# HGRN2 attention and a maxout FFN on one core: the order of weight copies, loads, packing and stores on two DMA queues, and other rooms for the weight sums

## The chip, the core and the metric

The kernel runs on one core of a Trainium2 chip. The metric is the device time of one execution in microseconds (us), the median of several runs. A core has a matrix engine (TensorE, here PE; its weight loads are shown as PEld), a vector engine (VectorE, DVE), a scalar engine (ScalarE, ACT), a general engine (GpSimd, POOL) and a synchronising engine (SyncE, SP). Each engine takes its instructions strictly in its own order. DMAs are issued by an engine as instructions in that order too; SPq and ACTq are the names in the profile for the queues of SP and ACT.

## The reference

```python
def _attn_ref(q, k, v, f_logit):            # 4 batches, 8 heads, 768 steps, 48 features
    f = 1.0 / (1.0 + np.exp(-f_logit))
    state = np.zeros((B, H, D, D))
    for t in range(S):
        state = f[:, :, t, :, None] * state + np.einsum('bhd,bhe->bhde', k[:, :, t], v[:, :, t])
        y[:, :, t] = np.einsum('bhd,bhde->bhe', q[:, :, t], state)

def _moe_ref(x, w1, w2, w3, w_out):         # x: 3072 x 384; w1..w3: 384 x 768; w_out: 768 x 384
    h = np.maximum(np.maximum(x @ w1, x @ w2), x @ w3)
    return h @ w_out
```

The output of the attention, transposed to tokens by 384 features, is the input x of the second part. The four weights are handed in as 64-bit floats and brought to 32 bits on the chip.

## The kernel before

The sequence is cut into chunks of 64 steps. One unit u holds one chunk of two batches (128 tokens) with all eight heads, so there are 24 units (0 to 23); the state of each pair of batches is carried from unit u to unit u + 2. Four units make a group g of 512 tokens, for which the FFN is run. The attention of unit u and the FFN of the group before it are woven together by hand: a loop over u calls the attention's steps, and between them `fill(ns)` draws so many nanoseconds of matrix work from a generator of the FFN. What is written first comes first on its engine; nothing is reordered.

**A unit's attention.** From unit 6 on (`BY_ROWS = 6`) the gates f, the keys k and the queries q are loaded for two units at once: `load(8)` fetches f, k and q of units 8 and 9, eight DMAs for each of the three (L183). `load_v` fetches v of one unit in two DMAs (L164). `sigmoids(u)` (ACT, L311) makes the gates from f. `scan(u)` (DVE, L329) forms the running products of the gates. `after(u)` turns k (DVE, `kt`, L296), copies the ends (POOL, L339) and multiplies (POOL, `kh`, L340). `before(u)` scans again (L347), turns q (DVE, `qt`) and multiplies (POOL, `qh`, L351). `carry(u)` (POOL, L357) decays the state. On PE follow `pairs(u)` (k against q, L392), `values(u)` (L411), `sums(u)` (the new state, L436, added by DVE in L444) and `finish(u)` (the part of the state, L500). `finish` copies the result in three pieces into the group's tile `xT` (ACT, L506). The tile has a fourth part whose rows belong into gaps of the first three: `pack` moves them there with two DMAs (L519), once for units 0 to 2 of a group and once for the last.

**The FFN of group 0** (`ffn_first`) works with plain products while the weights still arrive and are rounded to 32 bits (`round_to`; ACT, DVE and POOL). When all three are there, `place` copies the second and third, minus the first, from `w_in[1]` and `w_in[2]` into the tiles `placed[0]` and `placed[1]`, in the row order that `xT` has (ten DMAs for each, L454 and L461). `linear` multiplies the first weight with `w_out` on PE (L776); the product is copied by ACT (L780), and placed by ten more DMAs from `w_nat` to `w_lin`. `outputs(i)` for i = 0 to 3 then makes the four output tiles (PE, L563), each in one of the two PSUM banks of the pool `ps_f`, copied out by ACT (L567) and stored by two DMAs (L555).

**The FFN of groups 1 to 5** (`ffn`) saves products by working on sums and differences of halves. It needs `w_sum` and one difference of the placed weights (`mix_in`, four POOL instructions of 128 x 768), `w_mix` of `w_out` (`mix`, four of 128 x 576), `x_mix` of `w_lin` (`mix_x`, five of 128 x 192), and for each group the sums of its inputs (`sums_of_x`, five of 128 x 256, L854). `placed[2]` serves as `w_sum`, `w_in[2]` holds `w_mix`. The PE products of these parts stand in L870 and L631.

**DMAs and their counters.** Every DMA, whichever engine issues it, counts its completion on one of eight counters. The counter is chosen when the program is built, in the order in which the builder expects the DMAs to run. A DMA is issued only when the one before it on the same counter has landed; the issuing engine waits for that in front of the DMA instruction, beside whatever the data demands.

Of the kernel before, what the change touches and what calls it, by code (L numbers as in the profile page):

```python
# [9 lines left out]
FP32 = mybir.dt.float32  # L10
# [3 lines left out]
ALU = mybir.AluOpType  # L14
# [41 lines left out]
def kernel(  # L56
# [33 lines left out]
    def fast():  # L90
        ctx = ExitStack()
        with ctx:
# [455 lines left out]
            def new_top(w):  # L548
                return work.tile([128, TOK], FP32, name="top")[:, 0:w]

            def store(u, o):
                c, bp = divmod(u, 2)
                for a in range(2):
                    t0 = (2 * bp + a) * S + c * C
                    nc.sync.dma_start(out=out[t0:t0 + C, :], in_=o[a * C:(a + 1) * C, :])  # L555

            def outputs(hm, xT, i):
                p = bank()
                t = slice(i % 2 * UT, (i % 2 + 1) * UT)
                terms = [(hm[:, j, i * UT:(i + 1) * UT], w_out[:, j, :]) for j in range(NJ)]  # L560
                terms += [(by_halves(xT)[:, i // 2, k, t], w_nat[:, k, :]) for k in range(NK)]
                for n, (lhsT, rhs) in enumerate(terms):
                    nc.tensor.matmul(p[:, 0:DM], lhsT=lhsT, rhs=rhs, start=(n == 0), stop=(n == NJ + NK - 1))  # L563
                    if n % NK == NK - 1:
                        if n == NJ + NK - 1:
                            o = o_four[:, i]
                            nc.scalar.copy(o, p[:, 0:DM])  # L567
                            store(i, o)
                        yield NK * DM * COLUMN


# [2 lines left out]

            HJ, HD = NJ // 2, DM // 2
            corner = lambda k, n: w_out[:, k::2, n * HD:(n + 1) * HD]
            w_mix = [corner(0, 1)] + [w_in[2][:, :, n * HD:(n + 1) * HD] for n in range(4)]
            x_mix = [w_lin[:, 0, HD:]] + [w_mix[4][:, n] for n in range(2)] + [keep.tile([128, HD], FP32, name="mix")]
            s_mix = [w_in[1][:, n, :].rearrange("q (jj t) -> q jj t", jj=HJ) for n in range(NK)]
            s_last = keep.tile([128, HALF], FP32, name="s_last")  # L580
# [1 line left out]

            def mix(n):

                dst, x, y = ((w_mix[2], corner(1, 1), corner(0, 1)), (w_mix[0], corner(0, 1), corner(0, 0)),
                             (w_mix[1], corner(1, 1), w_mix[0]), (w_mix[3], corner(1, 0), w_mix[1]))[n]
                nc.gpsimd.tensor_tensor(dst, x, y, op=ALU.subtract)

            def mix_x(n):

# [172 lines left out]
            def turn(j):  # L763

                p = ps_f.tile([128, TOK], FP32, name="p")
                piece = w_in[0][:, :, j * 128:(j + 1) * 128]
                for a in range(NK):
                    nc.tensor.transpose(p[:, a * 128:(a + 1) * 128], piece[:, a, :], ident)
                nc.scalar.copy(piece, p[:, 0:DM].rearrange("q (a c) -> q a c", a=NK))
                yield DM * COLUMN  # L770
# [15 lines left out]
            def ffn_first(xT):  # L786
                hm = new_hm()
                steps = [(j, slice(n * HALF, (n + 1) * HALF)) for n in range(2) for j in range(J_HALF)]
                steps += [(j, slice(0, TOK)) for j in range(J_HALF, NJ)]
                n_step = 0  # L790
                for j, t in steps:
                    w = t.stop - t.start
                    for i in (1, 2):
                        p = yield from product(xT, j, i, t)
                        if i == 1:
                            nc.scalar.copy(hm[:, j, t], p)
                        else:
                            nc.vector.scalar_tensor_tensor(hm[:, j, t], hm[:, j, t], 0.0, p, op0=ALU.max, op1=ALU.max)
                        round_to(ROUNDED[n_step])
                        load_weights(2, rounded[0] - 1)  # L800
                        yield (1 if w == TOK else NK) * w * COLUMN
                        n_step += 1
                        if n_step in TURNED:
                            yield from turn(TURNED[n_step])
                for a in range(NK):
                    if a < 2:
                        for n in range(2 * NK + 2):
                            place(placed[a].bitcast(FP32), w_in[a + 1], n)
                    for cost in linear(a):
                        round_to(rounded[0] + 1)  # L810
                        yield cost
                for n in range(2 * NK + 2):
                    place(w_lin, w_nat, n)
                made = iter([lambda n=n: mix_in(n) for n in range(4)] + [lambda: mix(0)])
                for i in range(GRP):
                    for n, cost in enumerate(outputs(hm, xT, i)):
                        if i or n:
                            next(made, lambda: None)()
                        if i == GRP - 1 and n == 1 and 1 in packed:
                            sums_of_x(1)  # L820
                        if i == GRP - 1 and n == 2:
                            for k in range(1, 4):
                                mix(k)
                        yield cost


# [1 line left out]


            w_two = [t.bitcast(FP32) for t in placed[0:2]]  # L830
            w_sum = [placed[2].bitcast(FP32)[:, n] for n in range(NK)]

            def mix_in(n):

# [23 lines left out]
            def inputs_by_pairs(g, hm, xT):  # L858
# [57 lines left out]
                def fourth(n):  # L916
                    into(A[n], n, w_two[1][:, 1], t4)
                    yield COST
                    into(A[n], n, w_two[1][:, 2], t5)
                    nc.vector.scalar_tensor_tensor(out(n, 0), out(n, 0), 0.0, two(A[n]), op0=ALU.max, op1=ALU.max)  # L920
                    nc.vector.scalar_tensor_tensor(out(n, 1), out(n, 1), 0.0, u3, op0=ALU.max, op1=ALU.max)  # L921
                    sums_of_hm(hm, n)
                    if g == 1:
                        for i in ((0, 1), (2, 3, 4), ())[n]:
                            mix_x(i)
                    yield COST

                yield from start(0)
# [52 lines left out]
            with tc.manual_schedule():  # L981
# [78 lines left out]
                for u in range(GRP, NU):  # L1060
                    n = u + 1
                    part = EARLY if u < 2 * GRP else PART
                    if n == BY_ROWS:
                        scan(n)
                    fill(part)
                    keys(u)
                    keys_by_blocks(u, 2)
                    if u > GRP:
                        finish(u - 1, xT)
                        if u % GRP == 3:  # L1070
                            pack(0, 2, xT)
                        elif u % GRP == 0:
                            pack(3, 3, xT)
                    if u % GRP == 0:
                        if u > GRP:
                            packed[u // GRP - 1] = xT
                            pending.append(ffn(u // GRP - 1, xT))
                        xT = x_tiles[u // GRP % 2]
                    pairs(u)

                    if u + 2 <= BY_ROWS:
                        load(u + 2)
                    if BY_ROWS <= u + 3 < NU and u % 2:
                        load(u + 3, one, "fkq" if u % GRP == 1 else "f")
                    if u + 2 < NU:
                        load_v(u + 2)
                    keys_by_blocks(u, 3)
                    if n < NU:
                        if n < BY_ROWS:
                            sigmoids(n)  # L1090
                        if n != BY_ROWS:
                            scan(n)
                    check_range(u - CHECKS, 0)
                    fill(part)
                    if n < NU:
                        after(n)
                        before(n)
                    fill(part)
                    if BY_ROWS < u + 2 < NU and u % GRP == 0:
                        load(u + 2, one, "k")  # L1100
                    values(u)
                    if n < NU:
                        carry(n)
                    check_range(u - CHECKS, 1)
                    fill(part)
                    if BY_ROWS < u + 2 < NU and u % GRP == 0:
                        load(u + 2, one, "q")
                    keys_by_blocks(n, 0)
                    fill(part - 1000 if u < 2 * GRP else part)
                    keys_by_blocks(n, 1)  # L1110
                    check_range(u - CHECKS, 2)
                    if u + 2 >= CHECKS:
                        check_load(u + 2 - CHECKS)
                    if BY_ROWS <= u + 2 < NU:
                        sigmoids(u + 2)
                fill(PART)
                finish(NU - 1, xT)
# [270 lines left out]
```

## Time and profile before

| | us |
|---|---|
| median of 3 runs | 415.52 (415.25 to 416.81) |
| the profiled execution | 416.47 |
| its span in the profile | 414.6 |
| PE busy | 397.8 (96% of the span) |
| DVE, POOL, ACT busy | 290.8, 245.2, 178.7 |

The span is the time from the first to the last instruction that the profiler saw; 1.9 us of the profiled execution lie outside it. Times inside the profile are counted from the span's start. A row such as `80.68 1.13 ACT L506 COPY xT<-y 128x256 f32<-128x256 f32 x3 [2.92 <-PE y L500]` says that three copies of line 506 began at 80.68, took 1.13 us from the first's start to the last's end, and that ACT had stood idle for 2.92 us until PE's line 500 released it. For SPq the duration is the time that issuing took; the time to landing comes on top.

### The profile page before, as it was taken

The numbers are of one execution on the slowest core, as the hardware profiler recorded it, in microseconds if no ns is written. First come the engines' busy times: TensorE is split into PE (matmuls) and PEld (weight loads), VectorE is DVE, ScalarE is ACT, GpSimd is POOL, SyncE is SP. The second block draws the span as 40 slices with busy tenths as digits, with TensorE's granted clock in tenths as the row PEclk, the third lists the DMA queues.
The fourth block names the chain that finished last, engine by engine and source line by source line (L and its number), as shares of the span: only waits on it lengthen the run. The fifth ranks groups of instructions, "written<-read, shape, count | busy, mean of one in ns | idle before, by whom it ended". The sixth has DMA issues, their size and how long they took to land.

```text
span 414.6 us, 11546 instructions
## 1 busy us (share of the span) xinstructions
PE 397.8 (96%) x4598; PEld 332.4 (80%) x4598; DVE 290.8 (70%) x569; ACT 178.7 (43%) x412; POOL 245.2 (59%) x270
## 2 busy tenths in 40 slices
PE   4988999999999999999999999999999999999995
PEld 4766775566668889998889988889988899988984
DVE  6987897996695899898888976988894550002500
ACT  2478786511223531444541354533345324576210
POOL 2189694730989887487496376667466860435700
PEclk9999999999999999999999999999999999999999
DMA  8989987677356767377625376724473011541002
GB/s 170 237 261 273 250 231 93 86 143 159 83 104 96 122 114 132 70 118 89 137 78 104 52 117 86 163 64 80 71 146 96 2 55 44 148 136 60 0 21 62
DMA packets 181562, 47.21 MB, mean 114 GB/s; under 512 B 160448, under 2 KB 179200, under 8 KB 181504
## 3 DMA queue, kind: packets, MB, share of 16 engines
q1 hardware_dynamic: 178032, 45.62, 54.0%
q10 hardware_dynamic: 3472, 0.81, 0.9%
q8 instruction: 37, 0.61, 0.6%
q14 instruction: 21, 0.17, 0.1%
HBM read 37.75 MB, written 4.72 MB: 102 GB/s over the span
## 4 chain that ended last, share of the span: by engine, by line
PE 76%; DVE 6%; SPq 5%; POOL 3%; DMA 3%; ACT 3%; issue 2%; ACTq 0%; POOLq 0%; DVEq 0%
PE p L870 16%; PE p L631 14%; PE tr L870 13%; PE tr L631 11%; PE p L537 6%; PE p L563 3%; PE y L411 3%; PE y L500 2%; PE p L776 2%; SPq L174 2%; DMA raw<-in_moe_w_dram 2%; PE a L392 2%; PE y L436 2%; DVE ks L382 2%; SPq L164 1%
## 5 line engine op out<-in xcount | busy, mean ns | idle before, releaser
L382 DVE STREAM_TRANSPOSE ks<-kh 32x128 f32<-32x128 f32 x256 | 77.4, 302 | 11.9 <-POOL kh L340 7.7
L870 PE MATMUL tr<-xT,placed 128*128 128x256 f32 x300 | 72.6, 385 | 0.3 <-DVE hm L913 0.3
L870 PEld LDWEIGHTS tr<-xT,placed 128*128 128x128 f32 x300 | 55.7, 190 | 9.3 <-ACT hm L878 1.2
L870 PE MATMUL p<-xT,placed 128*128 128x256 f32 x180 | 45.1, 382 | 0.3 <-POOL xT L854 0.3
L339 POOL COPY ends<-r 128x8 f32<-128x8 f32 x24 | 9.8, 407 | 48.5 <-DVE r L329 48.5
L870 PEld LDWEIGHTS p<-xT,placed 128*128 128x128 f32 x180 | 33.7, 190 | 5.3 <-POOL xT L854 0.7
L537 PE MATMUL p<-xT,w_in 128*128 128x256 f32 (+1 forms) x108 | 33.9, 458 | 3.0 <-POOL w_in L745 2.2
L329 DVE TENSOR_TENSOR_SCAN r<-gate,from_one 128x520 f32<-128x520 f32 x24 | 31.5, 1314 | 6.1 <-ACT gate L308 3.0
L340 POOL TENSOR_TENSOR kh<-kt,r 128x512 f32<-128x512 f32 x18 | 30.1, 1671 | 7.6 <-DVE kt L296 6.2
L639 DVE TENSOR_TENSOR o<-tr,w_in 128x384 f32<-128x384 f32 (+1 forms) x11 | 5.7, 521 | 38.6 <-PE tr L631 35.1
L347 DVE TENSOR_TENSOR_SCAN prod<-gate,from_inv 128x520 f32<-128x520 f32 x24 | 32.1, 1336 | 0.0
L603 POOL TENSOR_TENSOR w_in<-hm 128x256 f32<-128x256 f32 x15 | 11.1, 739 | 34.9 <-DVE hm L921 32.2
L506 ACT COPY xT<-y 64x256 f32<-64x256 f32 (+1 forms) x60 | 22.1, 369 | 19.2 <-PE y L500 18.1
L870 PE MATMUL p<-w_in,placed 128*128 128x256 f32 x120 | 30.0, 379 | 0.0
L913 DVE TENSOR_TENSOR hm<-tr,hm 128x512 f32<-128x512 f32 x15 | 10.3, 688 | 26.6 <-PE tr L870 19.7
L537 PEld LDWEIGHTS p<-xT,w_in 128*128 128x128 f32 x108 | 19.5, 190 | 11.8 <-issue 6.0
L636 ACT COPY w_in<-p 128x384 f32<-128x384 f32 x15 | 7.2, 478 | 46.0 <-PE p L631 46.0
L631 PE MATMUL p<-w_in,hm 128*128 128x192 f32 x120 | 25.4, 335 | 1.1 <-ACT w_in L636 1.1
L258 POOL TENSOR_TENSOR w_in<-top_bits,rest_bits 128x384 uint32<-128x384 uint32 x18 | 21.8, 1218 | 7.6 <-DVE top_bits L252 4.7
L280 ACT ACTIVATE raw<-top_bits 128x384 f32<-128x384 f32 x48 | 25.2, 526 | 0.4
L870 PEld LDWEIGHTS p<-w_in,placed 128*128 128x128 f32 x120 | 22.8, 190 | 3.1
L631 PE MATMUL tr<-w_out,w_in 128*128 128x192 f32 x120 | 24.4, 326 | 0.0
(159 smaller groups left out, 907.6 us busy)
## 6 DMA issues: line engine op xcount, KB each, us to landing
raw<-in_moe_w_dram SPq DMA_DIRECT2D x24, 384.0 KB, 3.8
v_ld<-in_v_dram SPq DMA_DIRECT2D x48, 96.0 KB, 3.2
placed<-in_moe_w_dram SPq DMA_DIRECT2D x12, 384.0 KB, 5.4
out_dram<-o SPq DMA_DIRECT2D x46, 96.0 KB, 2.2
placed<-in_moe_w_out_dram SPq DMA_DIRECT2D x6, 384.0 KB, 6.3
f_ld<-in_f_logit_dram SPq DMA_DIRECT2D x36, 64.0 KB, 3.4
k_ld<-in_k_dram SPq DMA_DIRECT2D x36, 64.0 KB, 2.5
q_ld<-in_q_dram SPq DMA_DIRECT2D x36, 64.0 KB, 2.5
```

Of the source, the lines that this page charges most:

```text
L258: nc.gpsimd.tensor_tensor(dst, by(top), by(rest), op=ALU.add)
L280: nc.scalar.activation(over, size, AF.Relu, scale=(-1 / HI_MIN, 1.0)[step - 1], bias=(1.0, -HI_END * (1 - 2.0 ** -24))[step - 1], accum_ou ...
L329: nc.vector.tensor_tensor_scan(r[:, 0:LEN][:, ::-1], flat(gate)[:, ::-1], flat(from_one)[:, ::-1], 1.0, op0=ALU.mult, op1=ALU.max)
L340: (nc.vector if u < BY_ROWS else nc.gpsimd).tensor_tensor(kh.rearrange("p h a t -> p a h t"), kt, by_batch(r[:, 1:LEN + 1].rearrange("p (x ...
L347: nc.vector.tensor_tensor_scan(flat(prod), flat(gate_tiles[u % 2]), flat(from_inv[u % 2]), 1.0, op0=ALU.mult, op1=ALU.max)
L382: nc.vector.transpose(ks[n * 32:(n + 1) * 32, :, par, e0:e0 + 32], kh[p0:p0 + 32, :, a, t0:t0 + 32])
L411: nc.tensor.matmul(y[o:o + DP, a, hp * C:(hp + 1) * C], lhsT=v_ld[s, 2 * hp + par, :], rhs=d["at"][s, par, hp, :], start=(hp == 0), stop=F ...
L506: nc.scalar.copy(xT[o, :, t0 + a * C:t0 + (a + 1) * C], y[i, a, 0:HP * C].rearrange("p (h t) -> p h t", h=HP))
L537: nc.tensor.matmul(p if w < TOK else p.rearrange("p (two t) -> p two t", two=2), lhsT=w_in[i][:, kt, j * 128:(j + 1) * 128], rhs=x[:, t.st ...
L563: nc.tensor.matmul(p[:, 0:DM], lhsT=lhsT, rhs=rhs, start=(n == 0), stop=(n == NJ + NK - 1))
L631: nc.tensor.matmul(b[:, p * HD:(p + 1) * HD], lhsT=x, rhs=w, start=id(b) not in begun, stop=True, skip_group_check=True)
L870: nc.tensor.matmul(b[:, j * HALF:(j + 1) * HALF], lhsT=w[:, (2 * n + j) * 128:(2 * n + j + 1) * 128], rhs=x, start=begin and j == 0, stop= ...
```

## The change

- In `ffn_first` the placing of both weights stands ahead of all of `linear` (before: each ahead of its own `linear(a)`). `mix(0..2)` and `mix_in(0..2)` are made during `linear(1)` and `linear(2)`, `mix_in(3)` at the first output, `mix_x` at outputs 2 and 3 (before: while group 1's inputs were multiplied), `mix(3)` at the last one.
- The rooms are swapped: `w_mix` lies in `placed[2]`, `w_sum` in `w_in[2]`. The second difference of `w_out` is formed from the first, by an addition.
- The stores of group 0's four outputs, and the packing of group 1's tile (at units 7 and 8), are issued by ACT instead of SP.
- `load(8)` moves from unit 5 to unit 6: f after `pairs(6)`, k and q and v of unit 8 after `values(6)`. `sigmoids(8)` moves from the end of unit 6 to unit 7, ahead of `scan(8)`.

```diff
-            def store(u, o):
+            def store(u, o, queue=nc.sync):
...
-                    nc.sync.dma_start(out=out[t0:t0 + C, :], in_=o[a * C:(a + 1) * C, :])
+                    queue.dma_start(out=out[t0:t0 + C, :], in_=o[a * C:(a + 1) * C, :])
...
-                            store(i, o)
+                            store(i, o, nc.scalar)
...
-            w_mix = [corner(0, 1)] + [w_in[2][:, :, n * HD:(n + 1) * HD] for n in range(4)]
+            spare = placed[2].bitcast(FP32).rearrange("q k c -> q (k c)")
+            w_mix = [corner(0, 1)] + [spare[:, n * NK * HD:(n + 1) * NK * HD].rearrange("q (k c) -> q k c", k=NK)
+                                      for n in range(4)]
...
-                dst, x, y = ((w_mix[2], corner(1, 1), corner(0, 1)), (w_mix[0], corner(0, 1), corner(0, 0)),
-                             (w_mix[1], corner(1, 1), w_mix[0]), (w_mix[3], corner(1, 0), w_mix[1]))[n]
-                nc.gpsimd.tensor_tensor(dst, x, y, op=ALU.subtract)
+                dst, x, y = ((w_mix[2], corner(1, 1), corner(0, 1)), (w_mix[1], w_mix[2], corner(0, 0)),
+                             (w_mix[3], corner(1, 0), w_mix[1]), (w_mix[0], corner(0, 1), corner(0, 0)))[n]
+                nc.gpsimd.tensor_tensor(dst, x, y, op=ALU.add if n == 1 else ALU.subtract)
...
+                for a in range(2):
+                    for n in range(2 * NK + 2):
+                        place(placed[a].bitcast(FP32), w_in[a + 1], n)
                 for a in range(NK):
-                    if a < 2:
-                        for n in range(2 * NK + 2):
-                            place(placed[a].bitcast(FP32), w_in[a + 1], n)
-                    for cost in linear(a):
-                        round_to(rounded[0] + 1)
+                    for n, cost in enumerate(linear(a)):
+                        round_to(len(pieces))
+                        if a:
+                            (mix, mix_in)[a - 1](n)
                         yield cost
...
-                made = iter([lambda n=n: mix_in(n) for n in range(4)] + [lambda: mix(0)])
                 for i in range(GRP):
                     for n, cost in enumerate(outputs(hm, xT, i)):
-                        if i or n:
-                            next(made, lambda: None)()
+                        if i == 0 and n == 0:
+                            mix_in(3)
+                        if (i, n) in ((2, 2), (3, 0)):
+                            for m in ((0, 1), (2, 3, 4))[i - 2]:
+                                mix_x(m)
...
                         if i == GRP - 1 and n == 2:
-                            for k in range(1, 4):
-                                mix(k)
+                            mix(3)
...
-            w_sum = [placed[2].bitcast(FP32)[:, n] for n in range(NK)]
+            w_sum = [w_in[2][:, n] for n in range(NK)]
...
-                    if g == 1:
-                        for i in ((0, 1), (2, 3, 4), ())[n]:
-                            mix_x(i)
...
                         finish(u - 1, xT)
+                        queues = act if u <= 2 * GRP else one
                         if u % GRP == 3:
-                            pack(0, 2, xT)
+                            pack(0, 2, xT, queues)
                         elif u % GRP == 0:
-                            pack(3, 3, xT)
+                            pack(3, 3, xT, queues)
...
-                    if BY_ROWS <= u + 3 < NU and u % 2:
-                        load(u + 3, one, "fkq" if u % GRP == 1 else "f")
-                    if u + 2 < NU:
+                    if u == BY_ROWS:
+                        load(u + 2, one, "f")
+                    elif u + 1 != BY_ROWS:
+                        if BY_ROWS <= u + 3 < NU and u % 2:
+                            load(u + 3, one, "fkq" if u % GRP == 1 else "f")
+                    if u + 2 < NU and u != BY_ROWS:
                         load_v(u + 2)
...
-                        if n < BY_ROWS:
+                        if n < BY_ROWS or n == BY_ROWS + 2:
                             sigmoids(n)
...
                     values(u)
+                    if u == BY_ROWS:
+                        load(u + 2, one, "kq")
+                        load_v(u + 2)
...
-                    if BY_ROWS <= u + 2 < NU:
+                    if BY_ROWS <= u + 2 < NU and u != BY_ROWS:
                         sigmoids(u + 2)
```

## The prediction, made before the changed kernel was run

> **What bounds the kernel now.** I read the page first: PE is busy for 96% of the span, so a change that leaves PE's work alone can save only PE's waits or add new ones. Then the list of who waited for whom on PE: between 60 and 340 us hardly any wait is long. Then the chain that ended last, between 105 and 155 us, and the timelines of SP, ACT and PE around it.
>
> ```profile
> PE 397.8 (96%) x4598; PEld 332.4 (80%) x4598; DVE 290.8 (70%) x569; ACT 178.7 (43%) x412; POOL 245.2 (59%) x270
> ```
>
> The chain runs over PE, except here:
>
> ```profile
> 109.89 0.13 SPq L519
> ...
> 118.70 2.00 DMA out_dram<-o
> 120.70 1.99 DMA xT<-xT
> 122.75 0.09 issue
> 122.84 0.74 POOL xT L854
> ```
>
> SP's queue is full: from 40 to 163 us one DMA follows another. The packing of unit 7, whose data ACT has copied by 109.9, is issued at 120.0; POOL waits for it, and PE's product of group 1 waits for POOL.
>
> ```profile
> 124.43 1.13 PE L870 MATMUL p<-xT,placed 128*128 128x256 f32 x4 [0.30 <-POOL xT L854]
> 131.32 0.71 DVE L296 STREAM_TRANSPOSE kt<-k_ld 128x512 f32<-128x512 f32 x1 [3.53 <-DMA q_ld<-in_q_dram]
> ```
>
> DVE waits for the keys of unit 10 for the same reason. How much it costs PE: from `pairs(9)` at 122.42 to `pairs(13)` at 183.94 are 61.52 us, over the next four units 59.62. The difference, 1.9 us, is all that a relief of this queue can give; of it I find 1.3 us in gaps between PE's products at 123.8, 138.0, 154.1 and 162.
>
> Two lines show the rule that matters most below: an engine's queue stands still behind a DMA that waits, here for up to 17 us.
>
> ```profile
> SPq L519 <- ACT xT L506: 64.7, 9, 17.0
> 94.59 1.14 ACT L506 COPY xT<-y 128x256 f32<-128x256 f32 x3 [1.55 <-PE y L500]
> 99.09 0.48 ACT L567 COPY o<-p 128x384 f32<-128x384 f32 x1 [3.36 <-PE p L563]
> 105.97 2.10 PE L563 MATMUL p<-w_out,hm 128*128 128x384 f32 x6
> 108.00 0.67 PE L500 MATMUL y<-qh,state 48*48 48x64 f32 x32
> 108.49 0.65 PE L392 MATMUL a<-qh,kh 48*64 48x64 f32 x32
> ```
>
> The second is `finish(6)`, after which unit 6 can be packed; the last is `pairs(8)`, which follows `finish(7)` with no gap. `qh(8)` is ready at 108.39, so `pairs(8)` has no slack at all.
>
> **What the Trainium skill says.** DMA: Bandwidth & Descriptors, Anatomy of one DMA: a semaphore is waited for on the issuing sequencer, before the DMA is dispatched; the trace agrees (the 17.0 us). The same page, Issuing engines are not separate DMA queues: a second issuing engine saves only the time of issuing, which the trace shows as 0.49 to 0.65 us a DMA on SP and 0.69 to 0.94 on ACT. TensorE: Matmul & The Clock Gate, Part 1: after an idle window of some 3.4 us PE's clock is halved until it was busy for about as long. The trace agrees at the start: four transposes take 0.87 us from 5.05 until about 10, and 0.43 us from then on.
>
> **What the change removes.** PE's list of instructions is the same in both programs, one by one; only rooms differ. SP loses eight stores and four packing DMAs, 12 x 0.62 = 7.4 us of issuing. POOL loses in 114 to 132 us four `mix` (7.5 us), and in 144 to 159 the five `mix_x` (3.1 us); they go to gaps, of which POOL has 4.3 us at 82 and 13.1 us at 91. If the loads kept their times, all 1.3 us of PE's gaps would go.
>
> **What it adds.** In the built order of the changed program the DMAs of two engines now share the eight counters. I followed each wait of the DMAs there to the DMA that it names:
>
> ```
> SP  placed[1], 8th and 9th of 10  wait for  ACT packing of units 4 to 6, both DMAs
> SP  k(8), 8th; q(8), 1st, 3rd, 5th  wait for  ACT's four stores of outputs 0 and 1
> ACT sigmoids(8)                   waits for  SP  all eight DMAs of f(8)
> PE  outputs(2), first product     waits for  ACT copy of output 0 (behind sigmoids(8))
> PE  finish(7)                     waits for  DVE new state, which stands behind qt(8)
> ```
>
> The first two are new: before, all those DMAs are on SP, each behind the one eight places ahead of it. The others cost nothing before, since f, k and q of unit 8 were issued by 85.5. SP's order is now: v(7), `placed[0]`, `placed[1]`, f(8), k(8), q(8), v(8), `w_lin`. So the loads of units 8 and 9 stand behind two DMAs that can't start until unit 6 is packed. Step by step, with issue times from SP's timeline:
>
> 1. SP ends v(7) at 70.8, issues ten DMAs of `placed[0]` and seven of `placed[1]` at 0.63 us each (5.04 for eight), and stops at 81.6.
> 2. ACT ends the copies of `finish(6)` at 94.59 + 1.14 = 95.7. It can't be earlier, since PE and ACT have no reason to be ahead. Packing is issued at 95.8 and 96.4 and lands 2.6 us after issue (the median of the rows of 72 KB): 98.4 and 99.0. SP has stood still for 17 us.
> 3. SP issues the last three of `placed[1]` until 100.3, then eight of f(8): 5.2 us (110.75: 5.16 for eight), until 105.5. The last starts at 105.0 and lands 2.8 us later: 107.8.
> 4. ACT waits there since 97; `sigmoids(8)` ends at 108.4, the copy of output 0 (ready at 99.1 before) at 108.9. PE, which wanted the bank at 105.97, loses 2.9 us. ACT issues two stores, copies output 1 at 110.7, issues two more; the four start at 108.9, 109.6, 110.7 and 111.4.
> 5. SP issues seven of k(8) by 109.2. The eighth waits for the first store: 108.9 + 2.2 (landing of stores) = 111.1. q(8) then runs at 111.8, 112.3, 112.9, 113.4, 113.9, 114.5, 115.0 and 115.5, and has landed at 115.5 + 2.5 = 118.0.
> 6. `qt(8)` on DVE 0.7 (118.7), `qh(8)` on POOL 1.2 (119.9), `pairs(8)` at 120.0 in place of 108.49: **11.5 us late**. `finish(7)` is late with it: its state is added at 119.2. PE stands still from 110.9.
> 7. An idle stretch of over 8 us halves PE's clock. By the page some 3.4 us run at half pace (1.7 us lost), by the start of this trace 5 us (2.5 us lost). I take 2.0.
> 8. Against it the 1.3 us of gaps: POOL now has the five `mix_x` (3 us) ahead of `sums_of_x` and is ready at about 136.6, PE wants it at 124.0 + 13.5 = 137.5, so that gap is gone. The keys of unit 10: SP ends `w_lin` at 123.7, f(10) at 129, v(9) and v(10) at 131.5, k(10) at about 138.5 (it waits for group 0's last stores) and lands at 141; DVE had them at 131.3 + 13.5 = 144.8. So those gaps go too: -1.3.
>
> PE is the bound from there to the end, so nothing is won back. Sum: 11.5 + 2.0 - 1.3 = +12.2. On the profiled execution: span 414.6 + 12.2 = 426.8, with the 1.9 us outside 428.7. That execution was 0.95 us over the median, 415.52; on the median I forecast **427.7 us**.
>
> **Costs at nothing.** The moved POOL work: `mix(0)` at 82 to 84.4, `mix(1)` and `mix(2)` behind `qh(7)` until 95, all before POOL is needed for unit 8; `mix_in` waits for `placed[1]` until about 104 and then runs 7.2 us to 111, ahead of `kh(8)`, whose keys come at 113.7. If the loads were on time, these 7.2 us would end by 103, 3 us before `kh(8)` is multiplied now. The other rooms cost as much as the old ones. ACT's issuing, 12 DMAs at 0.7 us: ACT is busy for a quarter of this stretch. Step 5's waits are its price, and bounded: without any wait on the stores q(8) would start right behind k(8), end at 113.9 and land at 116.4, `pairs(8)` at 118.4 (+9.9); with 0.9 us an issue on ACT and 3.0 us to landing (the row of ACT's own stores) q(8) lands about 2 us later (+13.5).
>
> **The rivals.**
> - *The queue is relieved and the waits don't bind* (faster). It needs f(8) to start at about 83.6, behind the 20 placing DMAs, with no halt; all loads then land by 102, `kh(8)` comes 2 us earlier, and 1.3 to 1.9 us go: 413.6 to 414.2. The point that decides: whether SP's 18th placing DMA starts near 82 or behind the packing at 95.8. For it: SP's backlog is real and on the chain. Against: the wait is in the program, and ACT can't pack earlier. 9%.
> - *Waits, but covered* (within 0.5%): the loads are late, yet PE has other products to run. Against it: PE is strictly in order, and `pairs(8)` has 0.1 us of slack. 3%.
> - *The delay repeats* (431 to 435). The stores on ACT hold SP again at k(10) and f(10), and unit 10's keys come late too. Step 8 finds 3.8 us of cover there; if the delays upstream are larger than I have them, the cover goes, and a second halt of 3 to 6 us comes: 15.2 to 18.2 over the median. 10%.
> - *The forecast's mechanism*, 78%: without stores' waits and with a clock that stays up 9.9 - 1.9 = +8.0 (423.5); with slow ACT issues, 2.5 us for the clock and no gap regained +16 (431.5).
>
> **How the numbers follow.** About 0.5%, 2.1 us, is what a measurement of this kernel tells from no change. Faster holds the first rival: 0.09. Same: 0.03. Slower: 0.78 + 0.10 = 0.88. The range 422 to 433 takes the forecast's own with a little more, and half of the third rival.
>
> **What would show it.** SPq: a halt from about 82 to 98 in the placing of `placed[1]`, released by the packing. ACT: `sigmoids(8)` at about 108, with the copy of output 0 right behind. PE: a first wait of 3 us at 106 for L567's copy, a second of over 8 us before L500, and products at half pace behind it. Units 9 to 13 at about 60 us instead of 61.5. Wrong: f(8) issued before 95, or `pairs(8)` before 112.

## The result and the profile after

| kernel | median (us) | range | runs | span of the profiled execution |
|---|---|---|---|---|
| before | 415.88 | 415.25 to 416.81 | 4 | 414.6 |
| after | 428.84 | 428.30 to 429.09 | 4 | 427.3 |

The ratio is 1.0308, with a 95% interval of 1.0284 to 1.0332: the change makes the kernel 3% slower. The profiled execution, 12.7 us longer in span, took 429.03 us.

The page of the changed kernel, busy times and granted PE clock (a digit for each fortieth of the span):

```profile
PE 399.1 (93%) x4598; PEld 332.9 (78%) x4598; DVE 288.0 (67%) x569; ACT 178.6 (42%) x412; POOL 244.8 (57%) x270
...
PEclk9999999999879999999999999999999999999999
```

PE has the same 4598 products and is busy for only 1.3 us more, so what was added is almost all waiting. The clock falls in two slices, from about 107 us on. PE's waits of the changed kernel (in us: total, number of times, longest) name two that the kernel before did not have:

```profile
PE y L500 <- DVE st L444: 9.3, 1, 9.3
...
PE p L563 <- ACT o L567: 2.2, 1, 2.2
```

L500 is `finish(7)`, which needs the state that DVE updates behind `qt(8)`; L563 is `outputs(2)`, which needs a bank that ACT's copy of output 0 empties. Behind both is SP. Its waits of the changed kernel, the two that were not there before:

```profile
SPq L461 <- DMA xT<-xT: 13.5, 2, 13.1
...
SPq L183 <- DMA out_dram<-o: 7.1, 3, 2.9
```

SP, whose placing DMA (L461) has nothing to do with `xT`, waits 13.1 us at one stretch for a packing DMA, and in the loads (L183) for stores. Its timeline (start, duration, instructions; a row's duration includes halts within it):

```profile
79.35 1.23 SPq L454 DMA_DIRECT2D placed<-w_in  x2
80.62 18.82 SPq L461 DMA_DIRECT2D placed<-w_in  x8
99.54 5.07 SPq L183 DMA_DIRECT2D f_ld<-in_f_logit_dram  x8
104.65 6.34 SPq L183 DMA_DIRECT2D k_ld<-in_k_dram  x8
111.04 4.93 SPq L183 DMA_DIRECT2D q_ld<-in_q_dram  x8
```

Eight DMAs of `placed[1]` take 18.82 us where those of `placed[0]` took 5.05. ACT's timeline of the same stretch:

```profile
94.07 1.14 ACT L506 COPY xT<-y 128x256 f32<-128x256 f32 x3 [2.08 <-PE y L500]
94.86 1.39 ACTq L519 DMA_DIRECT2D xT<-xT  x2
106.82 0.63 ACT L311 ACTIVATE sig<-f_ld 128x512 f32<-128x512 f32 x1 [11.61 <-DMA k_ld<-in_k_dram]
107.35 0.46 ACT L567 COPY o<-p 128x384 f32<-128x384 f32 x1
107.84 1.25 ACTq L555 DMA_DIRECT2D out_dram<-o  x2
```

ACT packs as soon as unit 6 is copied, then stands for 11.61 us until f(8) is there (the row names the load issued next, but `sig` reads `f_ld`), and the copy of output 0 with its store stands behind. The circle is closed: SP waited for ACT's packing, ACT for SP's load, and then SP's last DMA of k(8) and its first of q(8) for ACT's first two stores (2.2 us). The chain that ended last, between 80 and 125 us, runs over both meetings of the queues; SP issues within 0.04 us of the landing ("issue" is time in which nothing that the profile shows is waited for):

```profile
95.64 2.54 DMA xT<-xT
98.18 0.03 issue
98.22 0.59 SPq L461
...
108.47 2.55 DMA out_dram<-o
111.02 0.02 issue
111.04 0.53 SPq L183
```

On PE:

```profile
107.87 2.20 PE L563 MATMUL p<-w_out,hm 128*128 128x384 f32 x6 [2.25 <-ACT o L567]
119.39 1.11 PE L500 MATMUL y<-qh,state 48*48 48x64 f32 x32 [9.32 <-DVE st L444]
120.27 1.08 PE L392 MATMUL a<-qh,kh 48*64 48x64 f32 x32
121.28 3.47 PE L563 MATMUL p<-w_out,hm 128*128 128x384 f32 x6
```

Six products of L563 take 2.20 us before the 9.3 us of standing still and 3.47 after it, and the 32 products of `pairs(8)` take 1.08 us where those of the kernel before took 0.65: for a while PE runs at half its pace (below: the half clock).

The loss has one place. The starts of `pairs` (first product of L392) of each unit, in us from the span's start, with all the runs of the next section:

| run | unit 7 | unit 8 | unit 9 | 7 to 8 | 8 to 9 | 9 to 10 | 9 to 13 |
|---|---|---|---|---|---|---|---|
| before | 94.34 | 108.49 | 122.42 | 14.14 | 13.94 | 15.19 | 61.52 |
| after | 93.83 | 120.27 | 135.91 | 26.45 | 15.63 | 14.91 | 60.72 |
| packing and stores on SP | 94.70 | 108.85 | 122.78 | 14.14 | 13.94 | 15.35 | 61.38 |
| only stores on ACT | 94.11 | 115.52 | 131.36 | 21.40 | 15.84 | 22.31 | 67.12 |
| only packing on ACT | 94.22 | 117.58 | 133.31 | 23.36 | 15.74 | 14.70 | 60.64 |
| before, both on ACT | 94.10 | 127.10 | 143.35 | 33.00 | 16.25 | 14.93 | 60.38 |
| after, both on GpSimd | 93.89 | 108.04 | 121.97 | 14.14 | 13.94 | 14.70 | 59.51 |
| before, both on GpSimd | 94.69 | 109.60 | 124.03 | 14.91 | 14.42 | 16.86 | 61.76 |
| after, on SP, stores late | 94.08 | 108.23 | 122.16 | 14.14 | 13.94 | 14.70 | 59.51 |
| before, stores late | 94.22 | 108.37 | 122.30 | 14.14 | 13.94 | 14.70 | 59.51 |

From unit 13 on, the distances of before and after agree within 0.01 us.

### The profile page after: what moved, and what is told of

Read it like the earlier page. It is cut to its first block, busy times and chain, and to the rows that moved or that the text cites. A ratio compares the mean times of both kernels' runs of the same rounds, so it can differ in the third digit from the quotient of the medians.

```text
span 427.3 us, 11547 instructions
## 1 busy us (share of the span) xinstructions
PE 399.1 (93%) x4598; PEld 332.9 (78%) x4598; DVE 288.0 (67%) x569; ACT 178.6 (42%) x412; POOL 244.8 (57%) x270
## 4 chain that ended last, share of the span: by engine, by line
PE 77%; DVE 6%; SPq 4%; DMA 4%; issue 3%; ACT 2%; POOL 2%; ACTq 0%; DVEq 0%; POOLq 0%
PE p L875 15%; PE p L633 14%; PE tr L875 13%; PE tr L633 10%; PE p L537 6%; SPq L183 4%; PE p L563 3%; PE y L411 2%; PE y L500 2%; PE a L392 2%; PE p L778 2%; PE y L436 2%; DVE ks L382 2%; DMA out_dram<-o 1%; PE tr L291 1%
## 5 line engine op out<-in xcount | busy, mean ns | idle before, releaser
L875 PE MATMUL tr<-xT,placed 128*128 128x256 f32 x180 | 45.6, 386 | 0.2 <-DVE hm L918 0.2
L339 POOL COPY ends<-r 128x8 f32<-128x8 f32 x24 | 7.8, 327 | 57.9 <-DVE r L329 57.9
L340 POOL TENSOR_TENSOR kh<-kt,r 128x512 f32<-128x512 f32 x18 | 32.4, 1803 | 14.8 <-DVE kt L296 13.4
L875 PEld LDWEIGHTS tr<-xT,placed 128*128 128x128 f32 x180 | 33.2, 190 | 5.1 <-DVE hm L918 0.3
L329 DVE TENSOR_TENSOR_SCAN r<-gate,from_one 128x520 f32<-128x520 f32 x24 | 30.6, 1275 | 5.9 <-ACT gate L308 2.8
L875 PE MATMUL tr<-xT,w_in 128*128 128x256 f32 x120 | 31.3, 383 | 0.0
L347 DVE TENSOR_TENSOR_SCAN prod<-gate,from_inv 128x520 f32<-128x520 f32 x24 | 30.8, 1284 | 0.0
L875 PE MATMUL p<-xT,placed 128*128 128x256 f32 x120 | 29.6, 382 | 0.0
L633 PE MATMUL p<-placed,hm 128*128 128x192 f32 x120 | 25.4, 335 | 1.1 <-ACT w_in L638 1.1
L875 PEld LDWEIGHTS tr<-xT,w_in 128*128 128x128 f32 x120 | 22.4, 190 | 4.5 <-ACT hm L883 1.6
```

What stands on the lines that cost most here:

```text
L329: nc.vector.tensor_tensor_scan(r[:, 0:LEN][:, ::-1], flat(gate)[:, ::-1], flat(from_one)[:, ::-1], 1.0, op0=ALU.mult, op1=ALU.max)
L340: (nc.vector if u < BY_ROWS else nc.gpsimd).tensor_tensor(kh.rearrange("p h a t -> p a h t"), kt, by_batch(r[:, 1:LEN + 1].rearrange("p (x ...
L347: nc.vector.tensor_tensor_scan(flat(prod), flat(gate_tiles[u % 2]), flat(from_inv[u % 2]), 1.0, op0=ALU.mult, op1=ALU.max)
L633: nc.tensor.matmul(b[:, p * HD:(p + 1) * HD], lhsT=x, rhs=w, start=id(b) not in begun, stop=True, skip_group_check=True)
L875: nc.tensor.matmul(b[:, j * HALF:(j + 1) * HALF], lhsT=w[:, (2 * n + j) * 128:(2 * n + j + 1) * 128], rhs=x, start=begin and j == 0, stop= ...
```

## The experiments

Theory T is the prediction's: the DMAs that SP and ACT issue (in the kernels before and after, these two issue all of them) are counted by the same eight counters, so a DMA of SP's can't be issued before the one eight places ahead of it in the program, if that is ACT's, has landed. Rivals: R1, the loads of unit 8 are late because they were moved behind the weights; R2, issuing DMAs costs ScalarE itself the time; and, from the second group on, R3, any second queue does this.

**The queue undone, everything else kept.**

```diff
-                            store(i, o, nc.scalar)
+                            store(i, o)
...
-                        queues = act if u <= 2 * GRP else one
+                        queues = one
```

> The changed kernel with only the queue undone: packing and group 0's stores are issued by SP again, everything else (order of placing and loads, swapped rooms, earlier GpSimd work) stays as changed. Theory T (DMAs of SP's and ScalarE's queues wait for each other through shared completion counters): SP never stands between placing and the loads of unit 8, so placing ends about 86, q(8) is issued to about 99, pairs(8) starts near 108.5 as in the kernel before, and the time is 415 to 416.5. Rival R1 (unit 8's loads are late because they were put behind the weights): pairs(8) still starts at 118 or later, time 425 to 428. Rival R2 (ScalarE loses time by issuing twelve DMAs itself): about 415, so this run does not part R2 from T; the two halves do.

Measured: 415.28 us, ratio 0.9980 (0.9968 to 0.9992), `pairs(8)` at 108.85. R1 falls: the placing stands ahead of the loads here as well, and its timeline on SP runs through without a halt:

```profile
80.35 5.58 SPq L461 DMA_DIRECT2D placed<-w_in  x8
86.03 4.30 SPq L183 DMA_DIRECT2D f_ld<-in_f_logit_dram  x8
90.37 5.27 SPq L183 DMA_DIRECT2D k_ld<-in_k_dram  x8
95.69 4.20 SPq L183 DMA_DIRECT2D q_ld<-in_q_dram  x8
```

All the rest of the change, rooms, order and earlier GpSimd work together, is worth 0.1 to 0.3%.

**Half of it: only the stores on ACT.**

```diff
-                        queues = act if u <= 2 * GRP else one
+                        queues = one
```

> The changed kernel with packing back on SP's queue; group 0's eight stores stay on ScalarE's. Theory T: the halt of SP during placing is gone, but k(8)'s last and q(8)'s DMAs still wait for ScalarE's stores of outputs 0 and 1 (output 1's copy at about 106, its store landing near 109): pairs(8) starts about 115.7 (7.2 later than before), one stretch of PE at half clock 1.7, 0.8 regained: about 424. Rival R1: like the changed kernel, 428 to 429. Rival R2, by number of DMAs issued by ScalarE (eight of twelve): two thirds of the loss, about 424.5, with the time lost on ScalarE and not on SP; the wait rows of SP tell it from T.

Measured: 430.77 us, ratio 1.0360 (1.0339 to 1.0381), slower than the whole change and beyond every number expected. The first step came as theory T had it: `pairs(8)` at 115.52 (115.7 expected), and SP stands for stores, not ACT for its issuing. SP's waits between 68 and 135 us:

```profile
SPq L183 <- DMA out_dram<-o: 13.9, 4, 5.8
SPq L519 <- DMA out_dram<-o: 2.6, 1, 2.6
```

Two of the five waits I had not followed. f(10) waits 3.1 us for the store of output 2, and the packing of unit 7, now on SP again (L519), 2.6 us for the store of output 3. So packing is issued at 132.22; the same packing was issued at 119.37 with everything on SP. POOL's sums and PE's product of group 1 wait for it; PE's waits of this run:

```profile
PE y L500 <- DVE st L444: 6.8, 1, 6.8
...
PE p L875 <- POOL xT L859: 4.6, 1, 4.6
```

Units 9 to 10 take 22.31 us instead of 15.19; 4.6 us of that are the second wait, and behind it PE runs slowly once more: its products from 137.65 to 145.00 take 2.9 us longer than the same ones in the next run. The time alone lies nearest to R1's number; the start of `pairs(8)` and the waits of SP exclude R1.

**The other half: only the packing on ACT.**

```diff
-                            store(i, o, nc.scalar)
+                            store(i, o)
```

> The changed kernel with group 0's eight stores back on SP's queue; the four packing DMAs in question stay on ScalarE's. Theory T: SP stands from 81 to about 98.4 inside placing[1], since the completions of unit 6's packing come only after finish(6); after that nothing waits for ScalarE, q(8) is issued to about 113.5, lands 116, pairs(8) starts about 118.4 (9.9 later than before), half clock 1.7, 0.8 regained: about 426.5. Rival R1: 428 to 429, like the changed kernel. Rival R2, by number of DMAs (four of twelve): a third of the loss, about 420.

Measured: 426.18 us, ratio 1.0248 (1.0227 to 1.0269); `pairs(8)` at 117.58. Theory T has time and place; R2's 420 is out. SP's waits, 68 to 135 us:

```profile
SPq L461 <- DMA xT<-xT: 15.6, 2, 15.2
```

No wait for a store is left. Four packing DMAs alone bring 9.2 of the 12.3 us between units 7 and 8; the eight stores on top of them bring the other 3.1, where alone they brought 7.3. The two halts overlap: SP, late from the first, stands only 2.2 us for a store in the loads of unit 8 in the changed kernel.

**The queue alone, on the kernel before.** The same two lines, added to the kernel before, with its own order, rooms and GpSimd work:

```diff
-                            store(i, o)
+                            store(i, o, nc.scalar)
...
+                        queues = act if u <= 2 * GRP else one
```

> The kernel before with only the queue changed: packing of units 4 to 8 and group 0's stores on ScalarE's queue, the order of loads, the rooms and the GpSimd work as before. Theory T: the coupling alone makes it slower, since placing is spread between loads there and its DMAs share counters with packing of unit 7, which ends near 111: the input sums on GpSimd wait for placing until about 122, kh(8) stands behind them, pairs(8) starts near 127: 433 to 436. Rival R1 (the moved loads are the cause): about 415. Rival R2 (ScalarE issues the same twelve DMAs): the same loss as the changed kernel, 428 to 429.

Measured: 436.33 us, ratio 1.0500 (1.0464 to 1.0535), `pairs(8)` at 127.10. R1's 415 and R2's 428 to 429 are out. This is the strongest of the first four: the halt moves to where the counters put it. In the old order the DMA eight places behind the packing is one of q(8), not one of the placing (SP's timeline):

```profile
75.31 4.20 SPq L183 DMA_DIRECT2D k_ld<-in_k_dram  x8
79.55 19.22 SPq L183 DMA_DIRECT2D q_ld<-in_q_dram  x8
...
101.94 12.10 SPq L461 DMA_DIRECT2D placed<-w_in  x8
```

A second halt lies in the placing. SP waits there 6.6 us in all for group 0's stores, not for the packing of unit 7 as had been expected; the time came out close to the 433 to 436 expected, but on this point by another wait. GpSimd waits for the placing with `kh(8)` and `qh(8)` behind, and PE for GpSimd (GpSimd's waits; PE's timeline):

```profile
POOL placed L839 <- DMA placed<-w_in: 32.0, 1, 32.0
...
127.10 1.14 PE L392 MATMUL a<-qh,kh 48*64 48x64 f32 x32 [14.33 <-POOL qh L351]
```

So the change's other parts softened what its queue did: 428.84 against 436.33.

**Another second queue.** That every DMA shares the eight counters holds for those of SP and ACT. GpSimd's are counted, in the built program, by counters of their own, so the twelve DMAs can leave SP without being coupled to it.

```diff
-                            store(i, o, nc.scalar)
+                            store(i, o, nc.gpsimd)
...
-                        queues = act if u <= 2 * GRP else one
+                        queues = (nc.gpsimd, nc.gpsimd) if u <= 2 * GRP else one
```

> The changed kernel with the same twelve DMAs (packing of units 4 to 8, group 0's stores) issued on GpSimd's queue in place of ScalarE's; in the built program this queue's DMAs have completion counters of their own, so that no DMA of SP's waits for one of them. Theory T (it is the sharing of counters with ScalarE's queue): SP doesn't stand during placing or the loads of unit 8, pairs(8) starts within 1 us of 108.5, no half clock, time 414 to 416.5. Rival R3 (any second queue does this, since in-order waits for ScalarE's copies or contention between DMAs are what delays unit 8): pairs(8) late by 7 to 12, time 423 to 429. Third outcome: issuing DMAs costs GpSimd itself enough to delay kh(8) and qh(8), which would show as PE waiting for GpSimd and 417 to 420.

Measured: 414.19 us, ratio 0.9952 (0.9935 to 0.9968): faster than both kernels. R3 falls. SP's timeline has no halt, and q(8) is out 15.6 us sooner than in the changed kernel (100.4 against 116.0):

```profile
80.74 5.90 SPq L461 DMA_DIRECT2D placed<-w_in  x8
86.73 4.30 SPq L183 DMA_DIRECT2D f_ld<-in_f_logit_dram  x8
91.08 5.08 SPq L183 DMA_DIRECT2D k_ld<-in_k_dram  x8
96.21 4.21 SPq L183 DMA_DIRECT2D q_ld<-in_q_dram  x8
```

GpSimd pays for it in its own stream, 0.52 to 0.63 us a DMA (timeline of GpSimd, same run):

```profile
101.54 1.26 POOL L519 DMA_DIRECT2D xT<-xT  x2
102.79 0.21 POOL L339 COPY ends<-r 128x8 f32<-128x8 f32 x1
102.95 1.19 POOL L340 TENSOR_TENSOR kh<-kt,r 128x512 f32<-128x512 f32 x1
104.23 1.18 POOL L351 TENSOR_TENSOR qh<-qt,prod 128x512 f32<-128x512 f32 x1
105.34 1.14 POOL L555 DMA_DIRECT2D out_dram<-o  x2
```

Here `qh(8)` is ready at 105.4 and wanted at 108.04, so the packing ahead of it is covered. GpSimd has this room because its sums of weights were made early. The next run has them late; it has the old order of loads and placing too, so that the early work alone is not shown to be the reason.

**The same queue on the kernel before.** The two lines as in the run before, in the old order.

> The kernel before with only those twelve DMAs moved, to GpSimd's queue: the twin of the run that moved them to ScalarE's and took 436. Theory T: no DMA of SP's waits for them, so placing is done in time and pairs(8) starts by 110: 414.5 to 418. Rival R3: 430 or more, as on ScalarE's queue.

Measured: 418.36 us, ratio 1.0039 (1.0012 to 1.0066); a little over the upper end, and 18 us under ScalarE's queue in the same place. With the GpSimd work late, its DMAs now stand between that work and what PE waits for (PE's timeline):

```profile
109.60 0.69 PE L392 MATMUL a<-qh,kh 48*64 48x64 f32 x32 [0.58 <-POOL qh L351]
...
127.44 1.13 PE L870 MATMUL p<-xT,placed 128*128 128x256 f32 x4 [1.66 <-POOL xT L854]
```

**Only later stores, no second queue.** Group 0's stores go into the list from which group 1's are issued later on SP; first in the changed kernel with everything on SP, then as the only edit of the kernel before.

```diff
-                            store(i, o)
+                            late.append((i, o))
```

> The changed kernel with packing on SP and group 0's stores on SP too, but issued later, with those of group 1 (kept in the list that group 1's stores use). If SP's backlog from 100 to 135 us is what is left to gain in the changed order, the eight stores (some 5 us of SP) leave it: 413.5 to 415. If the gaps there are not SP's, no difference to the run with both on SP (415.3).

> The kernel before with only one edit: group 0's stores are put into the list that group 1's stores use and issued later on SP. Same question as the run above in the old order: 414.5 to 415.5 if SP's backlog there costs the gaps of units 9 to 12 (1.3 to 1.9 in all), 415.9 if it does not.

Measured: 414.17 us, ratio 0.9949 (0.9929 to 0.9969), and 414.24 us, ratio 0.9947 (0.9928 to 0.9967). The second is 0.26 us under its expected 414.5. In the kernel before, the keys of unit 10 were late because six stores stood ahead of them. SP's timeline of the kernel before:

```profile
117.38 2.50 SPq L555 DMA_DIRECT2D out_dram<-o  x4
119.97 1.35 SPq L519 DMA_DIRECT2D xT<-xT  x2
121.38 1.36 SPq L164 DMA_DIRECT2D v_ld<-in_v_dram  x2
122.83 1.23 SPq L555 DMA_DIRECT2D out_dram<-o  x2
124.16 5.05 SPq L183 DMA_DIRECT2D k_ld<-in_k_dram  x8
```

DVE's timeline of the last run, with late stores in the old order:

```profile
128.63 0.71 DVE L296 STREAM_TRANSPOSE kt<-k_ld 128x512 f32<-128x512 f32 x1 [0.17 <-DMA q_ld<-in_q_dram]
```

That transpose waited 3.53 us in the kernel before. Three different kernels (GpSimd's queue, late stores in the new order, late stores in the old) come out at 14.14, 13.94, 14.70, and 59.51 us for units 9 to 13, and within 0.1 us of each other in time: the relief of SP gave 2.0 us over these units in each, and the simplest edit has it.

## Why the prediction was right, step by step

- **The waits bind** (the forecast's mechanism): right, and shown by undoing the queue alone (-13.6 us in the median) and by doing it alone (+20.3).
- **Steps 1 and 2**, SP's halt: the halt was forecast to end the placing at 100.3 and ended it at 99.44. 0.5 of the 0.9 us between them is an earlier start: `finish(6)` came at 94.07 in place of 94.59, and unit 7 starts anywhere from 93.8 to 94.7 in the ten traces. The halt was 13.1 us long at one stretch where I had 17: the placing began at 72.8, not at 70.8, so SP came to the halt later. That miss cost nothing, since ACT's packing sets the end of the halt and not its start.
- **Steps 3 and 4**, f(8), `sigmoids(8)`, output 0: f(8) all issued at 104.6 (105.5), `sigmoids(8)` ended at 107.45 (108.4), the copy at 107.8 (108.9). PE's wait for the bank was 2.25 us (2.9).
- **Steps 5 and 6**: q(8) issued until 115.97 (about 116.0), `qt(8)` at 118.18 (118.0), `pairs(8)` at 120.27 (120.0). From unit 7 to unit 8 12.3 us were added where I had 11.5; 0.5 of the difference is that earlier start of unit 7. Step 5's lower bound, without any wait on the stores, was +9.9 at `pairs(8)`; the run with only the packing on ACT gave +9.2. PE's last wait ends through the state, as step 6 has it.
- **Step 7**, the half clock: 15.63 - 13.94 = 1.7 us, where I took 2.0. This equals the estimate from the Trainium skill (TensorE: Matmul & The Clock Gate, Part 1), some 3.4 us of work at half pace, but by chance. PE was slow already in `finish(7)`: from its start to that of `pairs(8)` passed 0.88 us, against 0.49 in the kernel before. With these 0.4 us PE lost 2.1, so that by estimate the half pace held for twice that, 4.2 us, between the page's 3.4 and the 5 of the start of the trace. The 0.4 did not count, since `pairs(8)` had to wait for `qh(8)` until 120.15. Where PE stood right in front of `pairs(8)` (the kernel before with both on ACT), the whole price came behind it: 16.25 - 13.94 = 2.3.
- **Step 8**, the gaps: 61.52 - 60.72 = 0.8 us regained, where I had 1.3. The mis-sized term is the end of f(10), forecast at 129: it came at 131.5, since the last of its DMAs waits 2.9 us for a store of output 2 on ACT, which I had not followed; k(10) ended at 141.4 in place of 138.5. The margin was misread too. I set the keys' landing at 141 against 144.8, when DVE would take them as late as before. But its row of the kernel before, with 3.53 us of waiting ahead of 131.32, says that it stood ready from 127.8; with the 13.5 us this is 141.3. So the gaps could go only with 0.3 us to spare, not 3.8. DVE then waited for the keys again, with 2.18 us:

```profile
143.35 0.71 DVE L296 STREAM_TRANSPOSE kt<-k_ld 128x512 f32<-128x512 f32 x1 [2.18 <-DMA k_ld<-in_k_dram]
```

That this wait is what kept the other 1.2 us of the 2.0 is likely (with late stores in the old order it was 0.17 us), but no run undid it alone.

- **All that there is to regain**, put at 1.3 to 1.9: 2.0 by the three faster kernels.
- **The sum**: -0.5 (the earlier start) + 12.3 + 1.7 - 0.8 = +12.7 in span, forecast +12.2; 428.84 in the median, forecast 427.7. Each term is within 0.8 us of its forecast, so the sum is not a balance of large errors.
- **The rivals.** The relief without a halt is what GpSimd's queue gave, at its 413.6 to 414.2 (414.19). The second halt is what the stores alone on ACT gave (430.77): whether the delay repeats hangs on where the packing stands, and I had given that case 10% on the size of upstream delays and the cover of 3.8 us, not on the next packing's own wait. "Covered" never showed.
- **Costs at nothing**: the rooms and the earlier GpSimd work are shown, together, by the run with everything on SP (415.28); they were not tried one by one. ACT's issuing is not part of that run. In the changed kernel its DMAs take 0.56 to 0.70 us each (half of the rows for two), and the copy of output 1, behind two of them, was done at 109.6, long before PE, held by the state, went on at 119.39.

What stays open: no run kept ScalarE's queue and changed its counters alone. That it is the counters rests on the waits in the built program, where the held placing DMA waits for nothing but the counter of a packing DMA; on the trace, in which it is issued right behind that DMA's landing; on the halts that moved to the DMAs which the counters name; and on GpSimd's queue, which differs from ScalarE's in more than the counters (the profile lists it as a software queue, the other two as hardware ones).

## What to carry to other kernels

A second queue for DMAs is not free when the two share completion counters: each DMA moved can hold the one eight places behind it on the other queue, and if the second engine in turn waits for the first one's loads, a short issue becomes a halt of some 13 us. List, in the built program, what each DMA waits for ahead of its data, before moving any to another engine. If a queue is only too full, first look for what in it is not urgent: deferring eight stores gave as much here as any other run.

## What had not been expected of the hardware

- The clock's price did not grow with the time that PE had stood still. After 6.3, 6.8, 9.3 and 14.3 us PE lost 2.2, 2.3, 2.1 and 2.3 us by slow products (0.4 us of the first three within `finish(7)`); after the 4.6 us of the run with only the stores on ACT it lost 2.9.
- GpSimd issued these DMAs at 0.52 to 0.63 us each (half of its rows for two), no slower than SP (0.49 to 0.65); `kh(8)` and `qh(8)` next to them took 1.19 and 1.18 us, as in the kernel before.
